# 48 matmuls on a page of zeros behind the last store of an FNet and FFN kernel

## The chip, the core and the metric

The kernel runs on one core of a Trainium2 chip. The metric is the device time of one execution in microseconds (us). Before the change it is 666.25 us, the median of two runs (665.85 and 666.64 us).

The engines have these names in the profile: PE is TensorE (the matmuls), PEld its weight loads, DVE is VectorE, ACT is ScalarE, POOL is GpSimd, SP is SyncE, which here only issues DMAs. A "q" behind a name (SPq, ACTq) is that engine's sequencer, which issues DMAs.

## The reference

The input x has 2048 rows of 512 elements. It is normalised over its rows and goes through a Fourier mixing written as matrix products, then through a feed-forward layer with 1792 hidden columns; each half adds its input back.

```python
def _A_ref(x, dft_seq_re, dft_seq_im, dft_hid_re, dft_hid_im):
    a = jnp.einsum("bsd,ed->bse", x, dft_hid_re)
    b = jnp.einsum("bsd,ed->bse", x, dft_hid_im)
    return jnp.einsum("ts,bse->bte", dft_seq_re, a) - jnp.einsum("ts,bse->bte", dft_seq_im, b)

def _B_ref(x, w1, w2):
    h = _silu(jnp.einsum("bsd,df->bsf", x, w1))
    return jnp.einsum("bsf,fd->bsd", h, w2)

h = x + _A_ref(_layernorm(x), ...)
h2 = h + _B_ref(_layernorm(h), B_w1, B_w2)
```

## The kernel before, in words

Every float32 operand of a product is split into a rounded high part and a remainder, both of the type fp32r. A product of two such operands is three matmuls (high by high, high by remainder, remainder by high) into one PSUM bank; the helper `three` issues them, so that nearly all matmuls carry the lines 316 to 318. ACT makes the high part (a Copy into fp32r, line 266), DVE the remainder (a subtraction, line 270). Most block products are done with seven instead of eight multiplications, which is why DVE and POOL add and subtract so many blocks (lines 714, 1208, 1223).

All matmuls of the kernel proper have 128 rows of weights by 128 columns, and a moving operand of 512 contiguous columns.

The stages follow each other on PE without a gap: the products with the sequence matrices (`plain`, `fast`), those with the hidden matrices (`mix_fast`), the first feed-forward product (`up`) and the second (`down`). The last one ends with bank `f4b`: its last half block is copied to an SBUF page in two pieces, by DVE (line 1265) and by ACT (line 1263), and each piece is stored by a DMA of its own (line 1266), one issued by SP, one by ACT.

The order of the work on each engine is written out. Each piece of work is appended to a list `events`, with a planned time in us, and its number is its place in that list when it was appended. At the end of `program` the list is sorted by planned time plus a correction, `MOVED.get(n, 0.0)`, which a table gives by the event's number n. The outer function then issues the events in that order, and each engine keeps it. So the table's corrections belong to numbers, not to names.

The last events appended before the change are two warm-ups on a tile `spare`, which take part in no result: `at(100, ...)`, a Silu on ACT (line 1353), whose table load so comes early, and `at(110, ...)`, a `partition_all_reduce` on POOL (line 1354), whose code so comes early. They have the numbers 1550 and 1551. The table has an entry for 1551 and none for 1550:

```python
    1537: 17.39, 1541: -0.02, 1549: 35.87,
    1551: 43,
```

so that before, the Silu is planned for 100 us and the reduction for 110 + 43 = 153 us.

SBUF pages (128 partitions by 1024 float32) come from a pool of 51 places, which a dry run of the program hands out; a new page takes the place that was freed first. PSUM is handed out in four buffers of two banks.

Before the first event, twelve bfloat16 matmuls on a page of zeros (`warm`) are issued, line 1357.

Of the kernel before, what the change touches and what calls it, by code (L numbers as in the profile page):

```python
# [7 lines left out]
F32 = mybir.dt.float32  # L8
BF16 = mybir.dt.bfloat16
F32R = mybir.dt.float32r  # L10
# [5 lines left out]
P = 128  # L16
# [166 lines left out]
class Plan:  # L183
# [5 lines left out]
    def page(self, name, dt=F32, shape=(2, 512)):  # L189
        self.taken.append(self.uses)  # L190
        self.last.append((self.uses, self.now))
        return Stub(self, len(self.taken) - 1)
# [14 lines left out]
def fnet_ffn_kernel(  # L207
# [18 lines left out]
    for plan.now, *_, f in program(stub, plan.page, stub, stub, stub, stub, x, xT, seq, hid, ffn, out):  # L226
        f()
    places = plan.places()

    def page(name, dt=F32, shape=(2, 512)):  # L230
        return pages.tile([P, *shape], dt, tag=f"pg{next(places)}", name=name)

    events = program(nc, page, keep, small, psum, dram, x, xT, seq, hid, ffn, out)


# [12 lines left out]
def program(nc, page, keep, small, psum, dram, x, xT, seq, hid, ffn, out):  # L248
# [11 lines left out]
    def banks(name):  # L260
        return psum.tile([P, 2, 512], F32, tag="ps", name=name)
# [70 lines left out]
    def at(t, f):  # L332
        events.append((t, 1, len(events), f))
# [1011 lines left out]
    up(1, 31, lambda: next(second[1]))  # L1345
    list(second[1])

    nc.vector.memset(warm, 0.0)
    nc.vector.memset(lower, -0.5 * EPS)
    nc.vector.memset(upper, EPS)  # L1350
# [43 lines left out]
```

## Time and profile before

| what | value |
|---|---|
| time, median of 2 runs | 666.25 us |
| the two runs | 665.85 and 666.64 us |
| span of the profiled execution | 664.2 us |
| median less that span | 2.05 us |
| PE busy | 657.6 us, 99% of the span |
| DVE busy | 575.7 us, 87% |
| ACT busy | 371.6 us, 56% |
| POOL busy | 97.8 us, 15% |
| share of PE in the chain that ended last | 98% |

The page gives the profiled execution's own time as its span alone, 664.2 us from the first to the last instruction; what lies around the span is taken from the runs as the 2.05 us of the table.

How to read it: busy time of PE counts a matmul from its start to the end of its results, and neighbouring matmuls overlap, so the number that matters for PE is the spacing of the starts. "Idle before" in a row is the time for which the engine stood still ahead of the instruction, with what released it. The granted clock (PEclk) is the share of full TensorE speed in a stretch.

### The profile page before, as it was taken

Reading aid. Unit: us, or ns where it says so; the run is one execution under the profiler, and the core shown is the slowest. Engines: PE = TensorE matmul, PEld = TensorE weight load, DVE = VectorE, ACT = ScalarE, POOL = GpSimd, SP = SyncE. Lnnn points to the kernel's source line nnn. Section 1 sums busy time; section 2 is a strip of 40 time slices with the busy share of each in tenths; the row PEclk is TensorE's granted clock in tenths of the full one; section 3 lists DMA queues with packets and bytes.
Section 4 is the critical chain, followed back from the end, with each engine's and each line's share of the span. In section 5 each row is a group of like instructions: output and inputs, shape, how many; then the busy total and the mean of one; then the engine's idle time right before and its main releaser. Section 6 shows DMA issues by size and latency. Waiting matters only on the chain.

```text
span 664.2 us, 8287 instructions
## 1 busy us (share of the span) xinstructions
PE 657.6 (99%) x2892; PEld 541.8 (82%) x2892; DVE 575.7 (87%) x727; ACT 371.6 (56%) x476; POOL 97.8 (15%) x128
## 2 busy tenths in 40 slices
PE   8999999999999999999999999999999999999997
PEld 5888888888888888888888888888888888888885
DVE  7999989898988999989999998988998854379964
ACT  6997456655445435364674555778543555664600
POOL 0011011111003434111121005343010000000000
PEclk9999999999999999999999999999999999999999
DMA  8981899999799586999999987669979645278803
GB/s 319 376 224 47 269 357 384 303 291 300 271 365 368 160 295 136 385 321 402 318 331 416 408 317 269 239 224 322 331 282 367 233 141 198 80 256 319 311 32 128
DMA packets 59706, 184.22 MB, mean 277 GB/s; under 512 B 6800, under 2 KB 13840, under 8 KB 59664
## 3 DMA queue, kind: packets, MB, share of 16 engines
q1 hardware_dynamic: 45456, 132.79, 54.8%
q0 software_dynamic: 13920, 50.63, 24.1%
q8 instruction: 23, 0.38, 0.3%
q10 hardware_dynamic: 288, 0.26, 0.1%
q14 instruction: 19, 0.16, 0.1%
HBM read 139.34 MB, written 44.32 MB: 277 GB/s over the span
## 4 chain that ended last, share of the span: by engine, by line
PE 98%; DMA 0%; DVE 0%; ACT 0%; issue 0%; DVEq 0%
PE m L317 11%; PE m L316 11%; PE m L318 11%; PE y L316 8%; PE y L318 8%; PE y L317 8%; PE f L318 6%; PE f L316 6%; PE f L317 6%; PE c L317 4%; PE c L318 4%; PE c L316 4%; PE vx L316 3%; PE vx L318 3%; PE vx L317 3%; PE c L517 1%
## 5 line engine op out<-in xcount | busy, mean ns | idle before, releaser
L266 ACT ACTIVATE ph<-raw 128x1024 fp32r<-128x1024 f32 x102 | 106.0, 1056 | 87.5 <-PE m L318 23.4
L270 DVE TENSOR_TENSOR pl<-raw,ph 128x1024 fp32r<-128x1024 f32 x88 | 112.1, 1289 | 9.1 <-ACT ph L266 7.1
L316 PE MATMUL m<-ph,S 128*128 128x512 f32 x192 | 74.7, 389 | 0.0
L317 PE MATMUL m<-pl,S 128*128 128x512 f32 x192 | 74.7, 389 | 0.0
L318 PE MATMUL m<-ph,S 128*128 128x512 f32 x192 | 74.7, 389 | 0.0
L316 PE MATMUL f<-gth,wf 128*128 128x512 f32 x161 | 62.6, 389 | 0.0
L317 PE MATMUL f<-gtl,wf 128*128 128x512 f32 x161 | 62.6, 389 | 0.0
L318 PE MATMUL f<-gth,wf 128*128 128x512 f32 x161 | 62.6, 389 | 0.0
L266 ACT ACTIVATE gth<-g 128x1024 fp32r<-128x1024 f32 x42 | 42.7, 1053 | 32.6 <-DVE g L1208 31.6
L270 DVE TENSOR_TENSOR gtl<-g,gth 128x1024 fp32r<-128x1024 f32 x42 | 50.3, 1219 | 7.0 <-ACT gth L266 5.7
L316 PE MATMUL m<-ph,X 128*128 128x512 f32 x144 | 56.0, 389 | 0.0
L317 PE MATMUL m<-pl,X 128*128 128x512 f32 x144 | 56.0, 389 | 0.0
L318 PE MATMUL m<-ph,X 128*128 128x512 f32 x144 | 56.0, 389 | 0.0
L1079 DVE TENSOR_TENSOR g<-vx,g 128x512 f32<-128x512 f32 x28 | 19.3, 689 | 30.5 <-PE vx L318 17.9
L714 DVE TENSOR_TENSOR raw<-raw,raw 128x1024 f32<-128x1024 f32 x36 | 43.9, 1221 | 0.5
L316 PE MATMUL y<-ph,hf 128*128 128x512 f32 x112 | 43.6, 389 | 0.0
L317 PE MATMUL y<-pl,hf 128*128 128x512 f32 x112 | 43.6, 389 | 0.0
L318 PE MATMUL y<-ph,hf 128*128 128x512 f32 x112 | 43.6, 389 | 0.0
L316 PEld LDWEIGHTS m<-ph,S 128*128 128x128 f32 x192 | 36.0, 188 | 7.5
L318 PEld LDWEIGHTS m<-ph,S 128*128 128x128 f32 x192 | 36.0, 188 | 7.5
L317 PEld LDWEIGHTS m<-pl,S 128*128 128x128 f32 x192 | 36.0, 188 | 7.4
L317 PEld LDWEIGHTS f<-gtl,wf 128*128 128x128 f32 x161 | 30.2, 188 | 6.3
(407 smaller groups left out, 1540.0 us busy)
## 6 DMA issues: line engine op xcount, KB each, us to landing
raw<-in_seq SPq DMA_DIRECT2D x84, 512.0 KB, 6.8
hf<-fd SPq DMA_DIRECT2D x28, 512.0 KB, 7.3
wf<-wd SPq DMA_DIRECT2D x28, 512.0 KB, 5.8
wf<-wd SPq DMA_DIRECT2D x28, 384.0 KB, 5.4
sf<-sd SPq DMA_DIRECT2D x18, 512.0 KB, 6.0
raw<-in_seq POOLq DMA_DIRECT2D x16, 512.0 KB, 6.9
fd<-hf POOLq DMA_DIRECT2D x14, 512.0 KB, 7.8
w<-in_ffn SPq DMA_DIRECT2D x23, 256.0 KB, 5.2
```

The source lines that it names most:

```text
L266: nc.scalar.activation(hi, src, AF.Copy, scale=sign)
L270: nc.vector.tensor_tensor(lo, src, hi, op=ALU.subtract)
L316: nc.tensor.matmul(acc, wh, mh, start=first, stop=False, skip_group_check=on)
L317: nc.tensor.matmul(acc, wh, ml, start=False, stop=False, skip_group_check=on)
L318: nc.tensor.matmul(acc, wl, mh, start=False, stop=last, skip_group_check=on)
L517: nc.tensor.matmul(o, wl, mh, start=False, stop=last)
L714: nc.vector.tensor_tensor(o, a, b, op=ALU.subtract)
L1079: nc.vector.tensor_tensor(g[q, f][:, tau, :], src, g[q, f][:, tau, :], op=ALU.add)
```

## The change

A function `probe` is added and put into the list of events at 800 us, behind all others. It takes one more page of SBUF, has DVE write zeros into it, takes one more PSUM buffer and issues 48 matmuls on that page, six each of eight forms. In all of them the weights are read from the same page. The result is read by nobody and stored nowhere.

```diff
@@ -1345,6 +1345,22 @@
     up(1, 31, lambda: next(second[1]))
     list(second[1])
 
+    def probe():
+        b = page("probe", F32)
+        nc.vector.memset(b, 0.0)
+        b = b.rearrange("p a t -> p (a t)").bitcast(F32R)
+        o = banks("probed")[:, 0, :]
+        w = b[:, 512 : 512 + P]
+        two = b[:, :512].rearrange("p (a t) -> p t a", a=2)
+        lines = b[:, :512].rearrange("p (a t) -> p t a", t=16)
+        forms = [(w, b[:, :512], o), (w, b[:, :256], o[:, :256]), (w[:, :64], b[:, :512], o[:64]), (w, two, o),
+                 (w, lines, o), (w, b[:, :1].to_broadcast([P, 512]), o), (w, b[:, 1:513], o), (w, b[:, :512], o)]
+        for v, m, u in forms:
+            for _ in range(6):
+                nc.tensor.matmul(u, v, m, start=True, stop=True)
+
+    at(800, probe)
+
     nc.vector.memset(warm, 0.0)
     nc.vector.memset(lower, -0.5 * EPS)
     nc.vector.memset(upper, EPS)
```

The eight forms are, in their order:

1. 512 contiguous columns, 128 columns of weights.
2. 256 contiguous columns.
3. 512 contiguous columns, 64 columns of weights.
4. `two`: 512 columns, read alternately from two halves that lie 256 elements (1024 bytes) apart.
5. `lines`: 512 columns with 16 elements (64 bytes) from each to the next.
6. One column read 512 times.
7. 512 contiguous columns, beginning one element later.
8. The first form again.

The probe is appended ahead of the two warm-ups, so it has the number 1550 now, and the warm-ups have 1551 and 1552. The table of corrections is unchanged. The Silu so falls under the entry 1551 and is planned for 100 + 43 = 143 us, and the reduction under none and is planned for 110 us. All earlier events keep their numbers, and all earlier pages keep their places.

On PE, the end of the program (f4b is the last bank of the output, gth and gtl the high and low part of its moving operand, wf the weights):

```order
 L317 MATMUL f4b<-gtl,wf 128x512
 L318 MATMUL f4b<-gth,wf 128x512
-L1390 UNCONDITIONAL_BRANCH
+L1360 MATMUL probed<-probe 128x512 x6
+L1360 MATMUL probed<-probe 128x256 x6
+L1360 MATMUL probed<-probe 64x512 x6
+L1360 MATMUL probed<-probe 128x512 x30
+L1406 UNCONDITIONAL_BRANCH
```

The 48 matmuls stand behind the last matmul of the output; the first of them waits for DVE. On DVE the memset of the page is the only new instruction, and the last: it stands behind the copy of line 1265 and waits for nothing else.

On ACT, in the middle of the products with the sequence matrices (raw is a block of such a matrix, ph its high part; the numbers tell blocks apart):

```order
 L266 ACTIVATE ph<-raw_1316 128x1024
 L266 ACTIVATE ph<-raw_1314 128x1024
 L266 ACTIVATE ph<-raw_1220 128x1024
+L1369 ACT_TABLE_LOAD
+L1369 ACTIVATE spare<-spare 128x1
 L266 ACTIVATE ph<-raw_1312 128x1024
```

The table load and its Silu have come here from a place 33 ACT instructions earlier, before `ph<-raw_1040`.

On POOL, in the same stage (fd is the scratch in HBM to which the prepared hidden matrices hf are stored; the row of line 729 is a DMA that adds a block onto another):

```order
 L813 DMA fd_76<-hf_855 128x1024
 L813 DMA fd_76<-hf_1064 128x1024
+L1370 ISA
+L1370 ISA spare<-spare 128x1
 L813 DMA fd_76<-hf_1018 128x1024
 L729 DMA raw_942<-in_seq 128x1024
```

The warm-up reduction and the loading of its code (the two ISA rows) have come here from a place twelve DMAs further on, behind the last store to fd; four POOL DMAs that add blocks (line 729) now stand behind them and not ahead.

## The prediction

> **What bounds the kernel now.** I read the head of the page first, then the waits of PE, then the chain that ended last, and at the end the last microseconds in order of time.
>
> ```profile
> span 664.2 us, 8287 instructions
> PE 657.6 (99%) x2892; PEld 541.8 (82%) x2892; DVE 575.7 (87%) x727; ACT 371.6 (56%) x476; POOL 97.8 (15%) x128
> PE 98%; DMA 0%; DVE 0%; ACT 0%; issue 0%; DVEq 0%
> ...
> PE idle L1357 <- DVE upper L1350: 1.2, 1, 1.2
> PE c L513 <- DVE X L489: 0.5, 1, 0.5
> ```
>
> PE is the bound from end to end: 98% of the chain is PE, and the last two rows, all that its waits list, hold 1.7 us, both in the first 6 us. Behind these PE never stands still until its work is out. So nothing that another engine does earlier can gain more than 1.7 us, and what is put on PE behind its last matmul lengthens the program by what does not fit under the tail. The tail is this:
>
> ```profile
> 654.39 0.39 PE L316 MATMUL f4b<-gth,wf 128*128 128x512 f32 x1
> ...
> 658.93 0.39 PE L318 MATMUL f4b<-gth,wf 128*128 128x512 f32 x1
> 659.36 0.42 DVE L1265 COPY r<-f4b 128x256 f32<-128x256 f32 x1 [1.80 <-PE f4b L318]
> 659.81 0.33 SPq L1266 DMA_DIRECT2D out<-r  x1
> 659.81 0.38 ACT L1263 ACTIVATE r<-f4b 128x256 f32<-128x256 f32 x1 [26.87 <-DVE r L1265]
> 660.23 0.35 ACTq L1266 DMA_DIRECT2D out<-r  x1
> ...
> out<-r ACTq DMA_DIRECT2D x1, 128.0 KB, 2.7
> ```
>
> The columns of the first rows are start and duration in us. The last matmul starts at 658.93 and ends at 659.32. DVE's copy ends at 659.78. ACT's store is issued at 660.23 and lands 2.7 us later, at 662.93. The program closes at 664.2, so 1.27 us lie between the landing and the end. From 659.32 on PE has nothing to do.
>
> The first row gives the spacing too: the bank f4b has 21 matmuls, the first at 654.39 and the last at 658.93, so 20 steps in 4.54 us, 0.227 us each. A matmul's own 0.39 us is longer because neighbours overlap.
>
> **The start of the probe.** The page of zeros is written by DVE behind its last copy, so not before 659.78. The trace has one memset of a size worth comparing, at the start of the program:
>
> ```profile
> 0.85 0.27 DVE L1348 MEMSET warm<- 128x256 uint32 x1 [0.85 <-PEq L1387]
> ...
> 1.08 0.06 DVE L1350 MEMSET upper<- 128x1 f32 x1
> ...
> 1.18 2.31 PE L1357 MATMUL idle<-warm 128*128 128x512 bf16 x5 [1.18 <-DVE upper L1350]
> ...
> L1223 DVE TENSOR_TENSOR r<-r,p 128x1024 f32<-128x1024 f32 x10 | 12.1, 1220 | 0.1
> ```
>
> 256 elements took 0.27 us, so 1024 take 4 x 0.27 = 1.08 us. The upper bound is 1.22 us, what an addition over as many elements takes in the last row; the lower bound 0.27. I take 1.08, since the other memset is the nearest row. DVE then is done at 659.78 + 0.03 + 1.08 = 660.89 (0.03 us is the step from its copy to ACT's piece at 659.81). From DVE's last memset at the start (1.08 + 0.06 = 1.14) to the first matmul at 1.18 lie 0.04 us, so the first probe matmul starts at 660.93. PE stood idle for 1.6 us. Nothing else holds it: the page and the PSUM buffer that the probe takes were given up some microseconds before.
>
> **The eight forms.** Five of them are contiguous streams of 512 columns as far as the trace knows streams (the first, the eighth, that with 64 columns of weights, that with one column read again, that one element later): 30 x 0.227 = 6.81 us. Fewer columns of weights cannot make a stream of 512 columns shorter than the stream. For the form of 256 columns the bounds are half the spacing, 0.113, and all of it, 0.227. What could hold it up is the weight load, one for each matmul:
>
> ```profile
> L316 PEld LDWEIGHTS m<-ph,S 128*128 128x128 f32 x192 | 36.0, 188 | 7.5
> ...
> 5.88 0.30 PEld L513 LDWEIGHTS c<-ph,X 128*128 128x128 f32 x2 [0.96 <-ACT ph L478]
> ```
>
> One load takes 188 ns, but two behind each other took 0.30 us together, so the second began 0.11 us after the first: loads can follow at that rate. I take 0.113: 6 x 0.113 = 0.68 us.
>
> That leaves the two forms whose columns lie 1024 and 64 bytes apart, 12 matmuls. No matmul of this trace reads a moving operand with jumps, so no row prices it. The low end is 0.227, a jump costing nothing. The high end is the slowest stream of 512 columns in the trace, that of the twelve zero matmuls at the very start:
>
> ```profile
> 2.86 0.15 PEld L1357 LDWEIGHTS <-warm 128*128 128x128 bf16 x1 [0.28 <-issue]
> 3.29 0.15 PEld L1357 LDWEIGHTS <-warm 128*128 128x128 bf16 x1 [0.28 <-issue]
> 3.71 0.15 PEld L1357 LDWEIGHTS <-warm 128*128 128x128 bf16 x1 [0.28 <-issue]
> ```
>
> These steps are (3.71 - 2.86) / 2 = 0.425 us. I take the high end. This is a choice: a jump between elements can only add, every row at 0.227 has neighbours side by side, and a reader that delivers a column every 0.44 ns (0.227 us for 512) will hardly do so for elements that each lie apart. 12 x 0.425 = 5.10 us, against 2.72 at the low end. The Trainium skill speaks for a price here ("Advanced Engine Details and Errata", section "SBUF Cachelines"): accesses that stay in one line of 16 bytes run at full performance, and a different line for each access costs a penalty. It gives no factor for TensorE. Every element of these two forms is in a new line; those of the other forms share lines. No run here shows it yet.
>
> **The sum.** 6.81 + 0.68 + 5.10 = 12.59 us for 48 steps. The last matmul starts one step earlier, at 660.93 + 12.59 - 0.23 = 673.29, and ends 0.39 later, at 673.68. The close of the program is bounded by 0 and the 1.27 us that followed the last landing; I take 0.9, since that landing has its own wait to be closed and PE's end has not. The span is 674.6 us, 10.4 more than before. The stores are hidden under it: they land at 662.93. The median of the runs lies 2.05 us over the profiled span; put on top of the median, 666.25 + 10.4 = 676.7 us.
>
> **The two moved warm-ups.** The numbers of the events shift, so "all else stays" does not hold: ACT's table load and POOL's reduction change places, and what they pass has to be priced.
>
> ```profile
> 106.97 1.28 ACT L1353 ACT_TABLE_LOAD   x1
> 108.26 0.20 ACT L1353 ACTIVATE spare<-spare 128x1 f32<-128x1 f32 x1
> ...
> 145.39 2.01 ACT L266 ACTIVATE ph<-raw 128x1024 fp32r<-128x1024 f32 x2 [1.27 <-DVE raw L714]
> 148.63 1.06 ACT L266 ACTIVATE ph<-raw 128x1024 fp32r<-128x1024 f32 x1 [1.23 <-DMA raw<-in_seq]
> 150.32 1.06 ACT L266 ACTIVATE ph<-raw 128x1024 fp32r<-128x1024 f32 x1 [0.62 <-DVE S L409]
> ...
> 109.34 1.05 POOL L813 DMA_DIRECT2D fd<-hf  x2 [3.41 <-ACT spare L1353]
> 119.31 0.89 POOL L729 DMA_DIRECT2D raw<-in_seq  x1 [8.92 <-DVE pl L272]
> ...
> 150.82 0.80 POOL L1354 PARTITION_ALL_REDUCE spare<-spare  x1
> 156.69 0.58 POOL L1018 DMA_DIRECT2D sd<-wS1h  x1 [5.07 <-ACT wS1h L266]
> ```
>
> The load and its Silu take 1.48 us. At the new place ACT is done with the two roundings ahead at 147.40 and stood idle for 1.23 us; the block behind, ph<-raw_1312, starts 0.25 us later, and 0.62 us idle follow it before 150.32. So the delay is gone in one instruction. At the old place 1.48 us fall away, which lets ACT run earlier where PE did not wait for it: nothing.
>
> The reduction was issued at 150.82 and the next POOL row is at 156.69, so its cost, with its code, is at most 5.9 us, at least 0.80. At its new place, between the two stores of 109.34, it delays the second of them by that. The next row at 119.31 waited 8.92 us for DVE: both fit. What else is queued behind on POOL, the adding DMAs, waits for DVE. Both moves are priced at nothing on PE; if the covers failed, the price is up to 1.5 us (ACT), and 5.9 - 8.92 is negative, so nothing (POOL).
>
> **The rivals.**
>
> Jumps are free (28%). For it: the trace shows no case in which they cost. Then 12 x 0.198 = 2.4 us fall away: 674.3 us.
>
> The clock falls. The rows:
>
> ```profile
> 656.00:659.50 3.50, 3.32 (x15) 2.43 (x13) 1.70 (x3) 0.00 (x0) 0.00 (x0) 1.00 0.99 356
> 659.50:662.90 3.40, 0.00 (x0) 0.00 (x0) 0.28 (x1) 0.38 (x1) 0.00 (x0) 1.00 0.69 253
> 663.00:664.20 1.20, 0.00 (x0) 0.00 (x0) 0.00 (x0) 0.00 (x0) 0.00 (x0) 0.50 0.00 0
> ```
>
> The column behind the five engines is the granted clock: full through 3.4 us in which PE did nothing, half from 663.0 on. So idleness costs the clock here some 3.6 us after the last matmul, and the probe's pause is 1.6. The Trainium skill ("TensorE: Matmul & The Clock Gate", "Part 1: The HAM clock gate") has the same: half speed after an idle window of about 3.4 us. It adds that the window is free-running, so where it falls against the pause is chance. If a window holding 1.6 us of idleness were taken for an idle one, one stretch of about 3.4 us would run at half speed and cost 1.7 us: 678.4 us. Against it: that window is more than half busy.
>
> More forms are slow: the column read again, or the stream one element off, at 0.425 too. Each adds 6 x 0.198 = 1.2 us, both 2.4: 679.1 us. I give this and the fallen clock 15% together.
>
> Slower by more than 2% (12%): a jump costs not the slowest spacing of the trace but the reading of each element by itself. At four times the contiguous spacing, 0.908 us, the twelve matmuls take 10.9 us, 5.8 more: 682.5 us. It decides from 2.9 us over the forecast, which is a spacing of 0.425 + 2.9 / 12 = 0.67 us. A half clock through the whole probe comes to about the same: 30 x 0.198 + 6 x 0.113 = 6.6 us more, 683.3 us, and is part of these 12%. For it speaks only that nothing in the trace bounds a jump; against it, that PE's zero matmuls at the start did raise the clock, so zeros count as work.
>
> The rest does not stay as it is (3%): the moved warm-ups reach PE. With ACT's 1.5 us: 678.2 us.
>
> Faster (1%): the earlier ACT work at 107 us could only shorten waits that PE does not have.
>
> **How the numbers follow.** The forecast, jumps at about the slow spacing, has 41%, so 676.7 us. The range reaches from 673.5, free jumps with an instant close (674.3 - 0.9, rounded up), to 681.0, which takes in slow forms and a fallen clock together (676.7 + 2.4 + 1.7 = 680.8) and leaves out most of the 12% and some of the rest. 2% is 13.3 us, the threshold 679.6 us; it is about what a measurement of this kernel can tell from no change. Over it lie the 12%, and a part of the cases between 678 and 681, 7%: slower 0.19, within 0.80, faster 0.01.
>
> **What would show it.** In the profile after, the last matmul of f4b should end near 659.3, the memset take about 1.1 us, the first probe matmul start near 660.9, and the starts step by 0.227 for the first, third and sixth to eighth form, 0.11 for the second, and about 0.43 for the fourth and fifth. The span should end about 0.9 us behind PE. If the two jumping forms step by 0.227, the first rival holds. If the last f4b matmul ends more than 0.5 us later than before, or PE has a new wait between 107 and 160 us, the moved warm-ups matter. A granted clock under 1.00 behind 660 us would show the fallen clock.

## The result and the profile after

The changed kernel takes 676.17 us, median of two runs (676.16 and 676.18), the kernel before 666.25 us (665.85 to 666.64). The ratio is 1.0151, with a 95% interval from 1.0121 to 1.018: 9.9 us more. That is within 2%, but the interval lies clear of 1. The profiled execution took 676.18 us, with a span of 674.4 us.

The head of the page after:

```profile
span 674.4 us, 8386 instructions
PE 669.6 (99%) x2940; PEld 550.1 (82%) x2940; DVE 576.5 (85%) x728; ACT 371.5 (55%) x476; POOL 97.6 (14%) x128
```

PE has 48 matmuls and 48 weight loads more than before, DVE one instruction; ACT and POOL have their old count. The waits of PE (us in total, times, the longest) are those of before and two more:

```profile
PE probed L1360 <- DVE probe L1350: 1.7, 1, 1.7
PE idle L1373 <- DVE upper L1366: 1.2, 1, 1.2
PE c L513 <- DVE X L489: 0.5, 1, 0.5
PE c L517 <- DVE X L409: 0.2, 1, 0.2
```

The first row is the pause ahead of the probe. The last lies in the first ten microseconds; the start of the program varies by a few tenths of a microsecond from run to run (the first matmul of line 513 starts between 5.91 and 6.28 us in the traces of this study). The end of the program in order of time (start, duration), PE and then DVE:

```profile
659.45 0.39 PE L318 MATMUL f4b<-gth,wf 128*128 128x512 f32 x1
661.52 11.69 PE L1360 MATMUL probed<-probe 128*128 128x512 f32 x48 [1.68 <-DVE probe L1350]
...
659.87 0.42 DVE L1265 COPY r<-f4b 128x256 f32<-128x256 f32 x1 [1.80 <-PE f4b L318]
660.46 0.91 DVE L1350 MEMSET probe<- 128x1024 f32 x1 [0.16 <-issue]
```

The last matmul of the output ends at 659.84. The memset runs from 660.46 to 661.37, the probe from 661.52 to 673.21, and the span closes 1.19 us later.

How the forms step is read best from the weight loads, since a load precedes each matmul and runs one matmul ahead. A row with x6 holds six loads: five steps and the last load's own 0.19 us (0.13 with 64 columns of weights). The rows below are the loads that start together with the matmuls of the second, fourth, fifth, sixth and seventh form:

```profile
662.96 0.73 PEld L1360 LDWEIGHTS probed<-probe 128*128 128x128 f32 x6
...
665.05 1.27 PEld L1360 LDWEIGHTS probed<-probe 128*128 128x128 f32 x6
666.34 0.19 PEld L1360 LDWEIGHTS probed<-probe 128*128 128x128 f32 x1
666.76 0.21 PEld L1360 LDWEIGHTS probed<-probe 128*128 128x128 f32 x1 [0.23 <-issue]
667.19 0.21 PEld L1360 LDWEIGHTS probed<-probe 128*128 128x128 f32 x1 [0.23 <-issue]
...
668.93 1.30 PEld L1360 LDWEIGHTS probed<-probe 128*128 128x128 f32 x6 [0.23 <-issue]
670.25 1.38 PEld L1360 LDWEIGHTS probed<-probe 128*128 128x128 f32 x6
```

The fourth form, `two`, begins at 665.05 and the fifth at 666.34: six matmuls in 1.29 us, steps of (1.27 - 0.19) / 5 = 0.216 us. The fifth, `lines`, steps by 667.19 - 666.76 = 0.43 and takes until 668.93, 2.59 us. For all eight, from the starts of the matmuls to the nanosecond:

| form | forecast, us for six | measured | step, us |
|---|---|---|---|
| 1 contiguous | 1.36 | 1.44 | 0.31 once, then 0.2265 |
| 2 256 columns | 0.68 | 0.71 | 0.12 |
| 3 64 columns of weights | 1.36 | 1.38 | 0.230 |
| 4 `two`, 1024 bytes | 2.55 | 1.29 | 0.216 |
| 5 `lines`, 64 bytes | 2.55 | 2.58 | 0.433 |
| 6 one column | 1.36 | 1.33 | 0.219 |
| 7 one element later | 1.36 | 1.43 | 0.2365 |
| 8 contiguous | 1.36 | 1.37 | 0.228 |

The forecast gave both jumping forms one price. One of them costs almost twice a contiguous stream, the other less than a contiguous stream.

### The profile page after: what moved, and what is told of

It reads as the page before. It is cut to its first block, busy times and chain, and to the rows that moved or that the text cites. A ratio compares the mean times of both kernels' runs of the same rounds, so it can differ in the third digit from the quotient of the medians.

```text
span 674.4 us, 8386 instructions
## 1 busy us (share of the span) xinstructions
PE 669.6 (99%) x2940; PEld 550.1 (82%) x2940; DVE 576.5 (85%) x728; ACT 371.5 (55%) x476; POOL 97.6 (14%) x128
## 4 chain that ended last, share of the span: by engine, by line
PE 98%; DMA 1%; DVE 0%; SPq 0%; DVEq 0%; issue 0%
PE m L317 11%; PE m L316 11%; PE m L318 11%; PE y L316 8%; PE y L318 8%; PE y L317 8%; PE f L318 6%; PE f L316 6%; PE f L317 6%; PE c L318 4%; PE c L317 4%; PE c L316 3%; PE vx L316 3%; PE vx L318 3%; PE vx L317 3%; PE probed L1360 2%
```

## The experiments

What was open: which property of `lines` costs its factor and why `two` does not pay it; whether the moved warm-ups cost anything; from what pause the clock falls; and whether the quicker order of `two` is worth anything to the kernel itself.

### The moved warm-ups alone

```diff
-    at(800, probe)
+    at(800, lambda: None)
```

> The probe is replaced by an event that issues nothing, at the same place in the list, so that the two warm-ups move as they did in the change and nothing else is done. The prediction's theory, that both moves are covered: the time of the kernel before within 0.1% (666.25 us give or take 0.7), and PE waits only in the first 10 us. The rival, that the moved warm-ups reach PE: up to 1.5 us more, with a wait of PE between 107 and 160 us. The last matmul of f4b ended 0.51 us later in the changed kernel's profile than before; if the moves did that, it is 0.5 us later here too.

Measured: 666.66 us (ten runs) against 666.41 (13 runs), ratio 1.0003, 95% interval 0.9993 to 1.0012: no difference that these runs can tell. The event keeps its number, so both warm-ups move as in the change. PE's list of waits has one row, none from their stage:

```profile
PE idle L1359 <- DVE upper L1352: 1.2, 1, 1.2
```

The rows of the stage do show a small cost, though, which that list leaves out. The table load stands behind a rounding that began late here, after ACT had waited 1.45 us for a DMA. So the load delayed the next rounding, DVE waited for that one, and PE's steps came out longer (start, duration):

```profile
149.34 1.06 ACT L266 ACTIVATE ph<-raw 128x1024 fp32r<-128x1024 f32 x1 [1.45 <-DMA raw<-in_seq]
150.42 1.28 ACT L1355 ACT_TABLE_LOAD   x1
...
152.90 1.23 DVE L270 TENSOR_TENSOR pl<-raw,ph 128x1024 fp32r<-128x1024 f32 x1 [1.05 <-ACT ph L266]
...
156.42 0.39 PE L316 MATMUL m<-ph,S 128*128 128x512 f32 x1
156.78 0.50 PE L317 MATMUL m<-pl,S 128*128 128x512 f32 x1
```

From 156.42 to 156.78 are 0.36 us, 0.13 over the spacing; the step behind it is 0.11 over: 0.24 us together. In the changed kernel's profile the block was there without a wait. ACT's rows at the new place and then POOL's are:

```profile
148.81 1.28 ACT L1369 ACT_TABLE_LOAD   x1
...
150.76 1.06 ACT L266 ACTIVATE ph<-raw 128x1024 fp32r<-128x1024 f32 x1 [0.46 <-DVE S L409]
...
110.50 0.66 POOL L1370 PARTITION_ALL_REDUCE spare<-spare  x1 [0.19 <-issue]
...
119.03 0.88 POOL L729 DMA_DIRECT2D raw<-in_seq  x1 [7.43 <-DVE pl L272]
```

ACT still waits 0.46 us for DVE behind the warm-up, and POOL still 7.43 us: here both covers hold, with less to spare than before (0.62 and 8.92), and no step of PE between 107 and 160 us is longer. Of the seven traces with the moved warm-ups two show the longer steps at 156 us, this one 0.24 us and that of the long pause below 0.15 us. So the moves cost PE nothing or up to a quarter of a microsecond, as the DMA comes early or late; they gain nothing.

### All forms `lines`

```diff
-        forms = [(w, b[:, :512], o), (w, b[:, :256], o[:, :256]), ...
+        forms = [(w, lines, o)] * 8
```

> All 48 matmuls of the probe take the fifth form, 512 columns that lie 64 bytes apart. If the probe is paid in full, one step after the other, and that form costs 0.432 us a step however long it goes on, the 48 take 20.7 us in place of 11.5, so 9.2 us more than the changed kernel: 685.4 us, 2.9% over before. If the doubling were an effect of a few matmuls in a row (a dip of the clock, or a queue that runs empty), the steps would fall back to 0.227 and the time to about 677.

Measured: 685.37 us. Of the weight loads, the third and the last:

```profile
661.88 0.20 PEld L1359 LDWEIGHTS probed<-probe 128*128 128x128 f32 x1 [0.21 <-issue]
...
681.38 0.21 PEld L1359 LDWEIGHTS probed<-probe 128*128 128x128 f32 x1 [0.23 <-issue]
```

45 steps lie between them: 19.50 / 45 = 0.433 us. The price of `lines` is a rate, not the cost of a change of form, and the sum for the program holds with it.

### A ladder of distances

```diff
+        def woven(a):
+            return b[:, :512].rearrange("p (a t) -> p t a", a=a)
+        far = b[:, :544].rearrange("p (a t) -> p t a", t=17)[:, :16, :]
+        near = b[:, :512].rearrange("p (g a t) -> p g t a", a=2, t=16)
+        next_line = b[:, :512].rearrange("p (g a t) -> p g t a", a=2, t=4)
+        by_line = b[:, :512].rearrange("p (a t u) -> p t a u", a=2, u=4)
+        by_pair = b[:, :512].rearrange("p (a t u) -> p t a u", a=2, u=2)
+        swap = b[:, :512].rearrange("p (h m l) -> p l m h", h=2, l=2)
+        forms = [(w, b[:, :512], o), *[(w, woven(a), o) for a in (2, 4, 8, 16, 32, 64, 128, 256)],
+                 (w, far, o), (w, near, o), (w, next_line, o), (w, by_line, o), (w, by_pair, o), (w, swap, o),
+                 (w, b[:, :512], o)]
```

`woven(a)` reads `a` equal parts of the 512 columns in turn, so `woven(2)` is `two` and `woven(32)` is `lines`.

> The probe's eight forms are replaced by sixteen, six matmuls each, all of 512 columns: contiguous; eight forms that read in turn from a = 2, 4, 8, 16, 32, 64, 128, 256 equal parts of the 512 (neighbours 512/a elements apart, 1024 bytes down to 8); 32 parts 17 elements apart instead of 16; two parts 64 bytes apart; two parts 16 bytes apart; two halves in turn, four elements from each; the same with two from each; an order that exchanges the highest and lowest bit of the column number; contiguous again. In the changed kernel a = 2 stepped by 0.216 us, a = 32 by 0.43, contiguous by 0.227. Theory 1, each access to a new line of 16 bytes costs double: a = 2 to 128 and the far, near and adjacent parts 0.43, a = 256, pairs and fours about 0.22; the 0.216 already seen for a = 2 speaks against it. Theory 2, a few lines are held, and one no longer held is dear: a = 2, perhaps 4 and 8, 0.216, larger ones to 64 and the 17 elements 0.43, near and adjacent parts 0.216. Theory 3, the distance in bytes decides, 64 bytes being bad: near parts 0.43, 17 elements 0.216. The contiguous form's extra 0.011 us: if it comes from reading a line's four elements one after the other, halves in turn by fours step by 0.227, and the bit exchange, which never reads two neighbours in a row, by 0.216.

Measured (697.41 us in all), steps in us:

| order of columns | step |
|---|---|
| contiguous, first and last | 0.231, 0.227 |
| 2, 4, 8 parts in turn | 0.216, 0.283, 0.486 |
| 16, 32, 64 parts | 0.435, 0.434, 0.432 |
| 128 parts (16 bytes on at each step) | 0.461 |
| 256 parts (8 bytes on at each step) | 0.452 |
| 32 parts, 17 elements apart | 0.473 |
| two parts in turn, 64 or 16 bytes apart | 0.216 |
| the two halves in turn, by fours | 0.25 |
| the two halves in turn, by twos | 0.34 |
| 0, 256, 2, 258, ..., then the odd columns | 0.231 |

The rows of weight loads for 2 and 4 parts, two neighbours for 8, two for 256, and the two parts 16 bytes apart:

```profile
663.36 1.27 PEld L1368 LDWEIGHTS probed<-probe 128*128 128x128 f32 x6
664.65 1.60 PEld L1368 LDWEIGHTS probed<-probe 128*128 128x128 f32 x6
...
667.33 0.21 PEld L1368 LDWEIGHTS probed<-probe 128*128 128x128 f32 x1 [0.28 <-issue]
667.81 0.21 PEld L1368 LDWEIGHTS probed<-probe 128*128 128x128 f32 x1 [0.28 <-issue]
...
679.84 0.21 PEld L1368 LDWEIGHTS probed<-probe 128*128 128x128 f32 x1 [0.25 <-issue]
680.29 0.21 PEld L1368 LDWEIGHTS probed<-probe 128*128 128x128 f32 x1 [0.24 <-issue]
...
686.70 1.27 PEld L1368 LDWEIGHTS probed<-probe 128*128 128x128 f32 x6
```

The Trainium skill ("Advanced Engine Details and Errata", section "SBUF Cachelines") charges a penalty where each access is in a different line of 16 bytes, and asks for at least two hits on a line. Taken column by column in the order of the stream, both halves of that fail here. With two parts in turn every column is in another line than the one before it, and the step is the smallest of all, 0.216. With 8 bytes from column to column every line is hit twice in a row, and the step is 0.452. So theory 1 falls, and theory 3 with it; theory 2 misses the orders by twos and fours (0.34 and 0.25). The guess that the contiguous order pays for taking a line's four elements one after the other falls too: the order 0, 256, 2, 258, ... never does that, and is no quicker.

What fits is a fourth theory, formed on these steps: fp32r columns are read as if by two readers, one for the even and one for the odd places of the stream, and what counts is how many of its columns a reader takes in succession from one line of four. Two parts in turn give each reader four, and 0.216. The contiguous order gives two (0 and 2 to the one, 1 and 3 to the other), and 0.227. Steps of 8 bytes and more give one, and 0.43 to 0.47. A reader that changes between two lines, and returns to each, pays something between: 0.28 with four parts, 0.34 with halves by twos. With eight parts a reader goes round four lines and pays most of all, 0.486. The readers are a way to order the steps; no row shows them.

### The two readers tested

```diff
+        apart = b[:, :514].rearrange("p (a t) -> p t a", t=257)[:, :256, :]
+        back = b[:, :512].rearrange("p (g a t) -> p g t a", a=4, t=2)
+        inside = b[:, :512].rearrange("p (g h l) -> p g l h", h=2, l=2)
+        sixths = b[:, :384].rearrange("p (a t) -> p t a", a=6)
+        fours = b[:, :512].rearrange("p (g a t) -> p g t a", a=4, t=4)
+        forms = [(w, b[:, :512], o), (w, woven2, o), (w, apart, o), (w, back, o), (w, inside, o), (w, sixths, o[:, :384]),
+                 (w, fours, o), (wc, c[:, :512], o), (wc, c[:, :1024].rearrange("p (t a) -> p a t", a=2)[:, 0, :], o),
+                 (wc, c[:, :2048].rearrange("p (t a) -> p a t", a=4)[:, 0, :], o),
+                 (wc, c[:, :512].rearrange("p (a t) -> p t a", a=2), o), (w, b[:, :512], o)]
```

`c` is the page read as bf16, `wc` weights of bf16, `woven2` the form `two`.

> Twelve more forms, six matmuls each. Theory 4, formed on the first ladder: the even and the odd columns are read by two readers, and what counts is how often each reader, by itself, stays in a line of 16 bytes: four times in a row 0.216 us a step (two parts in turn), twice 0.227 (contiguous, since each reader sees every second element; the bit exchange too), once about 0.45 (a step of 8 bytes), with something between where a reader goes to and fro between two lines (a = 4: 0.283). It expects: two parts 257 elements apart 0.216; columns 0,2,1,3 of each four 0.227; columns 0,2,4,6,1,3,5,7 of each eight 0.28 to 0.45; four lines in turn (0,4,8,12,1,5,...) 0.28; six parts of 64 in turn, 384 columns, over 0.21 where free reading would be 0.16; bfloat16 contiguous 0.216 (four to a reader and line), bfloat16 every second element 0.227, every fourth 0.45, two bfloat16 halves in turn 0.216. Theory 2, a few lines held open whoever reads them: all forms that go between two neighbouring lines (0,2,4,6,1,3,5,7 of each eight) and four lines in turn at 0.216 to 0.227, bfloat16 every second or fourth element no dearer than float32 contiguous or every second.

Measured (684.61 us in all). The fp32r forms came as the fourth theory has them: two parts 257 elements apart 0.216; the order 0, 2, 4, 6, 1, 3, 5, 7, in which two accesses in succession share a line but each reader changes lines at every one, 0.34; the order 0, 2, 1, 3, 0.227 to 0.232, as contiguous; four neighbouring lines in turn 0.268; 384 columns in six parts 0.222 to 0.242, where 384 free columns would be 0.16. Theory 2 falls with the 0.34. The rows of 0, 2, 4, 6, 1, 3, 5, 7 and of 0, 2, 1, 3, and two neighbours of the last bf16 form:

```profile
665.39 1.89 PEld L1368 LDWEIGHTS probed<-probe 128*128 128x128 f32 x6
667.42 1.35 PEld L1368 LDWEIGHTS probed<-probe 128*128 128x128 f32 x6
...
678.16 0.10 PEld L1368 LDWEIGHTS <-probe 128*128 128x128 bf16 x1 [0.39 <-issue]
678.64 0.10 PEld L1368 LDWEIGHTS <-probe 128*128 128x128 bf16 x1 [0.39 <-issue]
```

For bf16 the contiguous stream took 0.216, every second column 0.226 and every fourth 0.452, as expected. The miss is the last: two halves of bf16 in turn step by 0.485, where two readers would give 0.216.

### What reads bf16

```diff
+        def halves_by(u):
+            return c[:, :512].rearrange("p (a t u) -> p t a u", a=2, u=u)
+        near = c[:, :512].rearrange("p (g a t) -> p g t a", a=2, t=8)
+        quarters = c[:, :512].rearrange("p (a t u) -> p t a u", a=4, u=2)
+        forms = [(wc, c[:, :512], o), *[(wc, halves_by(u), o) for u in (2, 4, 8, 16)], (wc, near, o), (wc, quarters, o),
+                 (wc, c[:, 1:513], o), (wc, c[:, :1].to_broadcast([P, 512]), o), (wc, c[:, :512], o)]
```

> Ten forms in bfloat16, 512 columns each, six matmuls each, for the one form of the second ladder that theory 4 missed (two bfloat16 halves, a column from each in turn: 0.485 measured where 0.216 was expected). Theory 4b: with bfloat16 a reader takes two neighbouring columns at once, as one word of 4 bytes, so that turns by single columns break every word, and turns by two are to bfloat16 what turns by one are to float32: halves by two 0.216, halves by four 0.25 to 0.34, near parts by one column about 0.45, four parts by two 0.28. Theory 4c: there are no two readers with bfloat16 at all and each change of line costs: halves by two about 0.34 or more, by four 0.3, by eight 0.25, by sixteen 0.23. In both, contiguous 0.216, the stream one column later 0.216 to 0.236, one column read again 0.216 to 0.22.

Measured (681.24 us in all): contiguous 0.216; the halves in turn by twos 0.271, by fours 0.227, by eights and sixteens 0.2155; neighbouring lines in turn by single columns 0.485; four parts by twos 0.438; one element later 0.216; one column 0.218. Two neighbours of the halves by twos, then the row of the halves by eights:

```profile
663.37 0.10 PEld L1365 LDWEIGHTS <-probe 128*128 128x128 bf16 x1 [0.17 <-issue]
663.64 0.10 PEld L1365 LDWEIGHTS <-probe 128*128 128x128 bf16 x1 [0.17 <-issue]
...
666.08 1.18 PEld L1365 LDWEIGHTS <-probe 128*128 128x128 bf16 x6
```

Neither of the two theories written down for this run had these numbers: 0.216 by twos falls, and the other's four numbers were too high. The data go with one reader for bf16: eight columns in succession from a line of eight 0.216, four 0.227, two 0.27 where it returns to the line after one other, and 0.44 to 0.45 where it does so after three others or not at all, one 0.485. The two types then agree in one number. Contiguous fp32r is 128 lines for each reader, and 0.227 / 128 = 1.77 ns a line; bf16 with every fourth column is 256 lines, and 0.452 / 256 = 1.77 ns; `lines` is 256 for each reader, and 0.433 / 256 = 1.69 ns. By this estimate a stream is as slow as its lines or as its 512 columns (0.216), whichever is longer. It was worked out afterwards from these rows, and no run was made to test it. It does not give the 0.2365 of fp32r one element later, nor the 0.219 of one column, nor what a line costs to which a reader returns: bf16 by single columns opens 512 lines in 0.485 us, 0.95 ns each.

### The faster order in the whole kernel

The order 0, 4, 1, 5, 2, 6, 3, 7 costs 0.216 where the contiguous order costs 0.227. This kernel is the one before, without a probe, with every moving operand read in that order. Nothing is left out. A stream's order is also the order of the results in PSUM, so the roundings that feed a later product undo it (applied three times, the order is the plain one).

```diff
+    def lanes(v):
+        return v.rearrange("p (g a t) -> p g t a", a=2, t=4)
...
+        if turned:
+            src = src.rearrange("p m (g a t) -> p (m g) t a", a=2, t=4)
+            h, l = (v.rearrange("p m (g t a) -> p (m g) t a", a=2, t=4) for v in (hi, lo))
...
+        mh, ml = lanes(mh), lanes(ml)
...
-            part["M", q, c, n], remainder = rounded(C[c, q, n], "p", -1.0 if c else 1.0)
+            part["M", q, c, n], remainder = rounded(C[c, q, n], "p", -1.0 if c else 1.0, turned=True)
...
-            T[n], remainder = rounded(raw.pop(("T", n)), f"T{n}")
+            T[n], remainder = rounded(raw.pop(("T", n)), f"T{n}", turned=True)
```

> The kernel before, without a probe, in which every matmul reads its moving operand in the order 0,4,1,5,2,6,3,7 of each eight columns (two neighbouring lines in turn, 0.216 us a step in the first ladder against 0.227 contiguous). Done three times this order is none, so the roundings of the second and third stage's moving operands read their source in the same order, and after the second and the fourth stage the columns stand as before; the output is the whole of the reference's. If the 0.011 us come from the reading of the moving operand, they are in every matmul of the kernel, whatever its data, weights and PSUM bank: 2880 x 0.0108 = 31 us less on PE, 635 us if DVE (576 us busy) and the DMAs keep up, 636 to 650 with some new waits of PE for them, since the written order was made for the old spacing. If they belong to the probe (zeros, one page, one bank), the spacing stays 0.227 and the time 666 us, or some us more for the roundings that read in steps.

Measured: 654.09 us (652.45 to 655.63, four runs) against 666.5, ratio 0.9815 with a 95% interval from 0.9789 to 0.9841. It is the fastest version here that computes the whole result, 12.4 us under the kernel before, and above the 636 to 650 us that were expected with some new waits. The interval is clear of 1; whether the gain is over 2% it leaves open. The head of its page, and then two of its matmuls, two steps apart:

```profile
span 652.0 us, 8304 instructions
PE 631.1 (97%) x2892; PEld 543.4 (83%) x2892; DVE 576.5 (88%) x741; ACT 379.1 (58%) x476; POOL 97.7 (15%) x128
```

```profile
560.01 0.38 PE L327 MATMUL vx<-T4h,wal 128*128 128x512 f32 x1
...
560.44 0.38 PE L326 MATMUL vx<-T4l,wah 128*128 128x512 f32 x1
```

The step is 0.43 / 2 = 0.215, and 2835 of the 2891 steps lie between 0.2145 and 0.2165 us. So the gain of 0.0108 us a matmul is there throughout; 2880 of them make 31.1 us, and the span fell by 664.2 - 652.0 = 12.2. The rest was lost again where PE waits: its list of waits sums to 15.2 us here and 1.7 before. The longest rows:

```profile
PE m L326 <- DVE pl L277: 5.5, 4, 1.6
PE c L325 <- ACT C L574: 1.3, 1, 1.3
PE y L325 <- DMA hf<-fd: 1.3, 1, 1.3
```

Counted as what PE's steps hold over the spacing, it is 21.0 us here and 2.4 before, which is nearly the whole difference of 31.1 - 12.2 = 18.9. Of it 11.2 us lie between 60 and 375 us and 4.8 between 375 and 500, where before has none. The windows of that stretch (length, then busy time of PE, PEld, DVE, ACT and POOL with counts, the granted clock, the DMA engines' share, GB/s), of this kernel and then of the one before:

```profile
60.00:375.00 315.00, 306.52 (x1410) 264.93 (x1409) 298.46 (x338) 179.02 (x198) 59.98 (x77) 1.00 0.91 317
...
60.00:375.00 315.00, 315.00 (x1391) 260.82 (x1391) 295.34 (x322) 170.79 (x194) 59.48 (x76) 1.00 0.91 312
```

DVE is busy for 298.46 of 315 us, 95%, and the longest wait is for its low parts (`pl`). It was busy for 94% before too, and PE did not wait; so there was little room for a faster PE.

### How much of that is DVE's load

The kernel of the last section without the 36 subtractions of DVE on line 714 of the kernel before, which form combinations of the sequence matrices; it computes from other numbers.

```diff
-            elif n == 6:
-                sub(o, b11, b22)
-            else:
-                sub(o, *{5: (b12, b11), 7: (b22, b12)}[n])
```

> The kernel of two lines in turn, with the 36 subtractions of line 714 of the kernel before left out (DVE's differences of blocks of the sequence matrices in the second, third and fourth product of the first stage), so what follows is computed from other numbers; 36 x 1.22 = 44 us of DVE's work are gone from the stretch of 60 to 360 us. That kernel's spacing gives 31 us and its time only 12, and its PE waits mostly for DVE there. If DVE's load in that stretch takes the rest, the waits of PE in it go and the time falls by 6 to 10 us, to 644 to 648 us. If the waits come from loads or from the order, it stays within 2 us of 654.

The same cut in the kernel before:

> The kernel before with the same 36 subtractions left out, as the counterpart: at the spacing of 0.227 us DVE keeps up, PE waits for nothing after the first 6 us, and so the time stays at 666 us (within 1 us) although DVE has 44 us less to do.

Measured: 649.41 us, 4.7 under the 654.09; and 666.60 us for the kernel before with the cut, beside 666.19. Each is a single run; the four runs of the faster order lie between 652.45 and 655.63. In the kernel before, where PE waits for nothing in this stretch, a lighter DVE is worth nothing; in the kernel with the faster order it is worth some 4.7 us. PE's longest row of waits is halved:

```profile
PE m L326 <- DVE pl L277: 2.7, 3, 1.6
```

What PE's steps hold over the spacing between 60 and 375 us fell from 11.2 to 7.5 us. So DVE's load is a part of it, and less than expected (644 to 648). The rest is open: what stays are single waits for DMA, ACT and DVE, in an order of work that was written for the old spacing; a new order was not run.

### A longer pause ahead of the probe

```diff
-        nc.vector.memset(b, 0.0)
+        for _ in range(8):
+            nc.vector.memset(b, 0.0)
```

> The changed kernel with the page of zeros written eight times in a row, so that PE stands idle for 1.68 + 7 x 0.91 = 8.1 us ahead of the probe in place of 1.68. In the kernel before, the granted clock was 1.00 for 3.6 us after PE's last matmul and 0.50 behind. If idleness sets the clock and 1.68 us were too short for it, as the prediction had it, the clock now falls before the probe starts, the first matmuls step by about 0.43 us in place of 0.227 for up to 3.4 us, and the time is 676.2 + 6.4 + 1.7 = 684.3 us. If work of another kind or the pages' zeros keep the clock up, the first form steps by 0.227 and the time is 682.6 us.

Measured: 685.83 us, beside 665.95 for the kernel before. Of PE's waits the first row, of DVE's timeline the second memset, and the windows around the pause:

```profile
PE probed L1361 <- DVE probe L1351: 10.0, 1, 10.0
```

```profile
661.67 0.91 DVE L1351 MEMSET probe<- 128x1024 f32 x1 [0.28 <-DVE probe L1351]
```

```profile
663.00:666.00 3.00, 0.00 (x0) 0.00 (x0) 2.44 (x3) 0.00 (x0) 0.00 (x0) 0.50 0.00 0
670.00:672.00 2.00, 2.00 (x5) 1.61 (x6) 0.00 (x0) 0.00 (x0) 0.00 (x0) 0.50 0.00 0
672.00:674.00 2.00, 2.00 (x11) 1.61 (x11) 0.00 (x0) 0.00 (x0) 0.00 (x0) 0.74 0.00 0
```

The pause came to 10.0 us, not 8.1, since each memset of the same page waits 0.28 us for the one ahead. These 1.96 us were not in the expected 684.3, and the time is 1.5 us above it. The clock was half from 662.81, 2.95 us after PE's last matmul ended (659.86), and full again from 673.05, 3.17 us after the probe began (669.88). The first form stepped by 0.427 in that time and took 2.70 us instead of 1.44. So the fallen clock is a real mechanism, and PE's zeros count as work.

A pause of 1.68 us did not set it off: in the changed kernel the first form stepped by 0.2265 behind its first step of 0.31. That is the evidence, and not the granted clock of 1.00 on its page, since that trace has no record of the clock.

The Trainium skill ("TensorE: Matmul & The Clock Gate", "Part 1: The HAM clock gate") puts the fall behind an idle window of about 3.4 us on a free-running grid. The traces agree with the grid: each whole stretch at one clock is a multiple of 3.413 us, 658.77 us (193 times) at full clock in the kernel before, 645.12 us (189) in that with the faster order, 10.24 us (3) at half clock here. So the record of the clock, which runs on behind the span, tells where the windows end, and the rows of PE how much matmul time the window ahead held:

| trace | end of the window, us | matmul time in it, us | clock behind it |
|---|---|---|---|
| the kernel before | 662.95 | 0 | half |
| the long pause | 662.81 | 0.46 | half |
| the faster order | 649.18 | 0.77 | half |
| the two readers tested | 684.03 | 1.02 | half |
| the faster order, lighter DVE | 644.53 | 1.44 | full |
| the moved warm-ups alone | 661.88 | 1.59 | full |
| the kernel before, lighter DVE | 661.02 | 2.44 | full |

In these rows a window with up to 1.02 us of matmuls lowered the clock, and one with 1.44 us did not. A window of 3.41 us that takes in the whole pause of 1.68 us still holds 1.73 us of matmuls. By these rows the changed kernel's clock stays up wherever the grid lies. That is worked out from the traces; no run was made to find the bound between 1.02 and 1.44 us.

## Why the prediction was right, and where it was not

The forecast was 676.7 us and the measurement 676.17. The agreement is closer than the steps deserve: four terms were off, and they nearly cancel.

- **The bound.** PE from end to end, and what is put behind its last matmul lengthens the program: right. The stores land under the probe.
- **The end of the old work.** Forecast at 659.32, measured at 659.84: +0.52 us. By the prediction's own sign (more than 0.5 us later) the moved warm-ups would matter, but the rows have it elsewhere: the first matmul of line 513 starts at 6.19 instead of 5.91, and the wait for X at line 517 adds 0.2, both ahead of all that moved. The kernel before with less work on DVE, whose warm-ups are in their old place, ends its last matmul at 660.05, with that first matmul at 6.23.
- **The pause.** 1.61 forecast, 1.68 measured. Its parts were off in opposite ways: the memset took 0.91 us instead of 1.08, while the hand-overs, priced at 0.03 and 0.04, took 0.16 (from DVE's copy to its memset) and 0.15 (from the memset to PE). Four times a small instruction counts its fixed part four times: one element took 0.06 us, 256 took 0.27 and 1024 took 0.91. Why the hand-over to PE is 0.15 here and 0.04 at the program's start stays open.
- **The contiguous forms.** 6.81 forecast, 6.95 measured for the five; 0.68 and 0.71 for the 256 columns, where the halved spacing was the right end.
- **The jumping forms: the step that failed.** "I take the high end. This is a choice: a jump between elements can only add." `lines` cost 2.58 us against the 2.55 forecast. `two` cost 1.29: 1.26 us under its price, and below the low end of 1.36 too. A jump did not add; it saved. By the fourth theory that is because it lets four columns of one line follow each other at each reader. The trace before had no row on this, and the rule of the Trainium skill, read column by column, pointed the wrong way for this form. That `lines` agrees with 0.425 is luck. The row it was taken from is that of zero matmuls at the program's start, and the next row of the same trace has the last four of the twelve, the same matmuls, at half that step:

```profile
4.14 0.77 PEld L1357 LDWEIGHTS <-warm 128*128 128x128 bf16 x4 [0.28 <-issue]
```

  The last load of the four takes 0.10 us, so a step is (0.77 - 0.10) / 3 = 0.22 us, and the record of full clock begins at 4.18. So 0.425 was a contiguous stream at half clock, as was the 0.427 of the long pause, and no price of reading.
- **The sum of the forms.** 12.59 forecast, 11.53 measured by the steps: -1.06.
- **The close.** 0.9 us chosen between 0 and 1.27; 1.19 measured: +0.29.
- **The time outside the span.** 2.05 forecast, 676.18 - 674.4 = 1.8 measured. The 2.05 set the median of two runs against the span of one of them; wherever time and span of the same execution are on record, 1.7 to 1.9 us lie between.

In the span that is -1.06 + 0.52 + 0.07 + 0.29 = -0.18, 674.4 for 674.6, and 0.27 less outside of it.

The rivals. Jumps free: half of it happened, one form of the two, which no case of the prediction held apart. The fallen clock did not happen. The long pause shows that it is real, and the table of windows that a pause of 1.68 us was too short for it wherever the window lay, so this was not left to chance as the prediction had it. Slower by over 2% needed 0.67 us a jumping matmul; the largest of all orders tried is 0.486. The moved warm-ups were priced at nothing, and in the changed kernel they cost nothing, but the working was off. It counted ACT's idle 1.23 us as cover for the table load. Those lie ahead of the rounding that starts at 148.63, and the load stands behind it, where 0.62 us were idle; the next rounding so comes 1.48 - 0.62 = 0.86 us later and not 0.25. In the changed kernel the DMA came in time and hid that; in the run of the moves alone it did not, and PE lost 0.24 us.

## What to carry to other kernels

Where a kernel is bound by fp32r matmuls, the order in which the moving columns are read is worth a trial. Here 0, 4, 1, 5, 2, 6, 3, 7 ran at 0.216 us for 512 columns where the plain order takes 0.227, and the whole kernel fell to 654.09 us from 666.5. Before hoping for the whole of such a gain, look at how busy the engines are that feed PE: 31.1 us were freed and 12.2 kept; a lighter DVE gave 4.7 more, and the rest is open. And a forecast that comes out right in the sum says little on its steps: compare each term.

## What the runs showed of the hardware that was not expected

- An fp32r stream in plain order is not the quickest that PE ran: 0.227 us for 512 columns in the kernel and 0.227 to 0.231 in the probes, against 0.2155 for bf16 and 0.216 for fp32r in the order above.
- The orders in which each column opens a new line can be the quickest (0.216) or the slowest (0.486): what orders these steps is how many of the even and of the odd columns, each for themselves, follow each other in a line. The steps of bf16 are not ordered so, but by all its columns together.
- A contiguous fp32r stream that begins one element later takes 0.2365 us for 512 columns, where bf16 shows nothing (0.216). One column read 512 times takes 0.219, and 0.218 with bf16. Both are unexplained.
- Memsets that write the same page one after the other wait 0.28 us for each other, as the seven of the long pause do.
- Half clock came 2.95 us after the last matmul's end in one run and 3.6 us in another. The clock changes at the end of windows of 3.413 us, and a window with 1.02 us of matmuls in it still lowered the clock.
